# Expert output tiles: scaled on ScalarE and summed in DRAM by accumulating transfers, instead of summed in SBUF on VectorE

## The chip, the core and the metric

The kernel runs on one core of a Trainium2 chip. The core has a matrix engine (TensorE, PE in the profile), a vector engine (VectorE, DVE), an activation engine (ScalarE, ACT), a general-purpose engine (GpSimd, POOL) and a queue engine (SyncE, SP). Each executes its own instruction list in order, and waits on semaphores for the others. Sixteen DMA engines move data between DRAM and the on-chip memory (SBUF). The metric is device time in microseconds (us) for one execution.

## The reference, cut to what matters

```python
attn_out = attention(q, k, v, p)              # two small softmax attentions, 4 x 8 heads
x = attn_out as a 2304 x 512 matrix           # tokens x model width
h = x @ w_in;  g = h * cos(h);  x = g @ w_out # first feed-forward layer, 2048 wide
P = exp(logits - max), 8 rounds of row and column scaling   # 2304 x 8 gate, logits = x @ w_gate
out = zeros(2304, 512)
for e in range(8):                            # eight experts, 1024 wide, all of them for every token
    h = maximum(x @ w1[e], 0)
    ye = h @ w2[e]
    out += P[:, e:e+1] * ye
```

The change is about the last line: how the eight experts' results are scaled by the gate column and added up.

## The kernel before

Everything is float32 split into a high and a low part, so that each product is three matmuls (high x high, high x low, low x high). The first part of the program (attention and the first layer) has its last matmul (L562) at 403.9 us. The rest is the expert part, and the change lies in it alone.

**Units.** An expert's 1024 hidden columns are done in two halves, so there are 16 units (`u` from `U1` to `NU - 1`; `e, half = divmod(u - U1, 2)`). A unit goes over five token blocks `j`: four blocks of 512 tokens (`j` = 0 to 3) and a rest of 256 tokens (`j == NJ`). In a block, `g1_steps` makes the hidden activations in seven steps `n` = 0 to 6, each a call of `g1_mult` (12 matmuls, L726) followed by small VectorE and ScalarE work (L734, L735, L750, L755); the rest block uses `g1_rest` (L795) in two steps. The second matmul of an expert is done by `out_tile`: 12 matmuls of 512 columns (L830 to L832) make one output tile of 128 tokens x 512. A unit has 18 tiles: four for each of four blocks, two for the rest. The tiles of a block are made one block later: those of block `j` stand between the steps of block `j + 1` (after steps 1, 3, 4 and 5), and the two tiles of the rest block stand in block 0 of the next unit, after steps 1 and 3.

**Where output is summed.** `acc` (two SBUF tiles, `acc0` and `acc1`) holds the sum of all experts. Expert 0 writes it (ScalarE copy L836 in the first half, a VectorE add L838 in the second). Each later unit adds onto it with one VectorE instruction per tile, `scalar_tensor_tensor` on L842: `acc = psum * prob[:, t, e] + acc`. At the first half of expert 1 a `tensor_scalar` (L841) scales what expert 0 left. The last unit also writes each tile to the output in DRAM from SP's queue: one transfer for a tile of a block (L848), four transfers of 32 rows for a rest tile (L851), since its rows lie in four places; the very last tile is done in two parts of 256 columns.

**What sets the order.** The order is written by hand (`tc.manual_schedule()`); every engine gets its instructions in the order in which the program's lines are executed. Output tiles rotate over three PSUM banks. SP's queue carries the loads: `x_load` (L660) brings the two parts of one operand of `g1_mult` from DRAM (2 x 256 KB); it is issued after each `g1_mult`, into one of four slots, for the fourth `g1_mult` after it. The weights of the next unit are loaded at block 1 (L675, 4 x 256 KB; L212, 2 x 512 KB).

**What GpSimd does.** In the expert part it makes the low parts of the weights: `put` (L683) and `comb` (L686) for the first weights, and `w2_split` (L221) for the second ones, each of whose high parts ScalarE writes first (L682, L220). In the loop below, the splits of weight rows 2 and 3 of a unit stand in block 0 after the tiles of step 3 and in step 5 (`n in (3, 5)`); they are first read by the first tile of block 0, in block 1 after step 1. GpSimd issues no transfers before.

Of the kernel before, what the change touches and what calls it, by code (L numbers as in the profile page):

```python
# [13 lines left out]
AF = mybir.ActivationFunctionType  # L14
ALU = mybir.AluOpType
# [11 lines left out]
NU = U1 + U2  # L27
# [4 lines left out]
NJ = 4  # L32
# [71 lines left out]
def tile_kernel(ctx: ExitStack, tc: tile.TileContext, qT, kT, v, pT, w_in, w_out, w_gate, w1, w2, out):  # L104
    nc = tc.nc
# [17 lines left out]
    prob = const.tile([P, NT // P, E], F32, name="prob")  # L123
# [350 lines left out]
    def acc_cols(o, n):  # L474
        i, o = divmod(o, NT * KD // 2)
        return acc[i][:, o:o + n]
# [325 lines left out]
    def out_g2(u, j, i):  # L802
        parts = 2 if u == NU - 1 and j == NJ and i == 1 else 1
        for part in range(parts):
            out_tile(u, j, i, part, DM // parts)

    def out_rows(j, i):
        if j < NJ:
            r = HC * (2 * j + i // 2) + P * (i % 2)
            return out[r:r + P]  # L810
        return out.rearrange("(c r) d -> c r d", r=HC)[4 * i:4 * i + 4, HT:HC]

    def out_tile(u, j, i, part, width):
        t = 4 * j + i
        e, half = divmod(u - U1, 2)
        o = part * width
        ps = bank[:, 4 + counts["bank"] % 3, 0:width]
        counts["bank"] += 1
        for f in range(4):
            wh, wl = w_sb[u, 2, f]  # L820
            p, q = divmod(f, 2)
            if j < NJ:
                hi, lo = h_sb[u, j][q, i // 2]
                c = HT * p + P * (i % 2)
            else:
                hi, lo = h_sb[u, j][None, p]
                c = HT * q + P * i
            a, bq = hi[:, c:c + P], lo[:, c:c + P]
            wh, wl = wh[:, o:o + width], wl[:, o:o + width]
            nc.tensor.matmul(ps, lhsT=a, rhs=wh, start=(f == 0), stop=False)  # L830
            nc.tensor.matmul(ps, lhsT=a, rhs=wl, start=False, stop=False)  # L831
            nc.tensor.matmul(ps, lhsT=bq, rhs=wh, start=False, stop=(f == 3))  # L832
        dst = acc_cols(DM * t + o, width)
        if e == 0:
            if half == 0:
                nc.scalar.copy(dst, ps)  # L836
            else:
                nc.vector.tensor_tensor(out=dst, in0=ps, in1=dst, op=ALU.add)  # L838
            return
        if e == 1 and half == 0:  # L840
            nc.vector.tensor_scalar(dst, dst, prob[:, t, 0:1], None, ALU.mult)  # L841
        nc.vector.scalar_tensor_tensor(  # L842
            out=dst, in0=ps, scalar=prob[:, t, e:e + 1], in1=dst, op0=ALU.mult, op1=ALU.add
        )
        if u == NU - 1:
            rows = out_rows(j, i)
            if j < NJ:
                nc.sync.dma_start(out=rows[:, o:o + width], in_=dst)  # L848
            else:
                for c in range(4):  # L850
                    nc.sync.dma_start(  # L851
                        out=rows[c, :, o:o + width], in_=dst[32 * c:32 * c + 32, :]
                    )

# [76 lines left out]
    with tc.manual_schedule():  # L933
# [181 lines left out]
        for u in range(U1, NU):  # L1115
            for j in range(NJ + 1):
# [16 lines left out]
                i = 0  # L1133
# [76 lines left out]
```

## Time and profile before

| | |
|---|---|
| median of three runs | 1965.75 us (1965.14 to 1967.0) |
| the profiled execution: its own time | 1966.81 us |
| the profiled execution: span of the trace | 1965.0 us |
| TensorE (PE) busy | 1929.4 us, 98% of the span |
| VectorE / ScalarE / GpSimd busy | 49% / 32% / 26% of the span |
| granted TensorE clock, mean | 0.995 of full speed |
| DMA traffic | 319.08 MB, 162 GB/s on average |

The span is what the hardware profiler recorded between the first and the last instruction; the execution's own time lies 1.81 us above it. A busy share over the whole span mixes the parts of the program. What the change is worth is read from the expert part, from 634.9 us (the first L842, first tile of expert 1) to the end.

### The profile page before, as it was taken

The page shows a single profiled execution, that of the slowest core. Times are in us where ns is not written, and L with a number is a line of the kernel's source. Part 1 is how long each engine was busy: PE and PEld are TensorE (multiplying, and loading weights), DVE is VectorE, ACT ScalarE, POOL GpSimd, SP SyncE. Part 2 cuts the span into 40 slices and gives each one's busy share as a digit, 9 for nine tenths or more (in the row PEclk, how much of TensorE's full clock was granted, in tenths as well). Part 3 has the DMA queues.
Part 4 walks back from the last instruction along what each step waited for, and adds up shares of the span by engine and source line. Part 5 has one row for each costly group of instructions (what it writes and reads, how often), then busy time and mean ns, then how long its engine had stood idle before and what let it go on. Part 6 is the DMA issues. An engine that isn't in the chain of part 4 may idle for free.

```text
span 1965.0 us, 32232 instructions
## 1 busy us (share of the span) xinstructions
PE 1929.4 (98%) x13241; PEld 1739.3 (89%) x13241; DVE 964.8 (49%) x1439; ACT 621.7 (32%) x1062; POOL 516.4 (26%) x414
## 2 busy tenths in 40 slices
PE   7999999988999999999999999999999999999998
PEld 4799999977899898999989989898989898889897
DVE  6867776655544544343434444444434443434343
ACT  5877776633222212121212122222222121212110
POOL 3445554611221212121212131212122221212100
PEclk9999999999999999999999999999999999999999
DMA  8411111288464646455555556464647373736373
GB/s 296 151 46 53 55 54 34 81 262 260 138 214 148 207 153 194 161 190 166 188 179 165 182 161 197 147 213 130 219 125 234 109 237 118 236 117 231 117 228 102
DMA packets 287891, 319.08 MB, mean 162 GB/s; under 512 B 18432, under 2 KB 265088, under 8 KB 287744
## 3 DMA queue, kind: packets, MB, share of 16 engines
q1 hardware_dynamic: 287744, 317.02, 50.1%
q8 instruction: 104, 1.70, 0.4%
q14 instruction: 43, 0.35, 0.1%
HBM read 297.55 MB, written 19.40 MB: 161 GB/s over the span
## 4 chain that ended last, share of the span: by engine, by line
PE 93%; DVE 2%; ACT 2%; DMA 1%; issue 1%; POOL 1%; SPq 0%; ACTq 0%; DVEq 0%; POOLq 0%
PE bank L726 32%; PE bank L830 13%; PE bank L831 13%; PE bank L832 13%; PE bank L562 9%; PE bank L795 5%; PE bank L503 1%; PE bank L505 1%; PE bank L504 1%; PE bank L440 1%; DMA xl<-xd 1%; DMA k<-kT 1%; PE bank L866 0%; DVE xl L618 0%; DMA xd<-xl 0%
## 5 line engine op out<-in xcount | busy, mean ns | idle before, releaser
L726 PE MATMUL bank<-xh 128*128 128x256 f32 x1792 | 508.5, 284 | 2.8 <-DMA xh<-xd 2.6
L726 PE MATMUL bank<-xl,xh 128*128 128x256 f32 x1792 | 507.0, 283 | 1.6 <-DMA xl<-xd 1.6
L726 PE MATMUL bank<-xh,xl 128*128 128x256 f32 x1792 | 506.9, 283 | 0.0
L842 DVE SCALAR_TENSOR_TENSOR acc<-bank,prob,acc 128x512 f32<-128x512 f32 (+1 forms) x253 | 189.4, 749 | 364.4 <-PE bank L832 364.1
L726 PEld LDWEIGHTS bank<-xh 128*128 128x128 f32 x1792 | 340.9, 190 | 17.9 <-issue 4.7
L726 PEld LDWEIGHTS bank<-xl,xh 128*128 128x128 f32 x1792 | 341.1, 190 | 11.7 <-DMA xl<-xd 2.2
L726 PEld LDWEIGHTS bank<-xh,xl 128*128 128x128 f32 x1792 | 341.7, 191 | 0.0
L683 POOL TENSOR_TENSOR xl<-wraw,xh 128x512 fp32r<-128x512 f32 x128 | 167.2, 1321 | 649.0 <-ACT xh L682 469.2
L830 PE MATMUL bank<-whi,hreg 128*128 128x512 f32 (+1 forms) x822 | 324.0, 394 | 0.0
L831 PE MATMUL bank<-wlo,hreg 128*128 128x512 f32 (+1 forms) x822 | 323.6, 394 | 0.0
L832 PE MATMUL bank<-whi,hreg 128*128 128x512 f32 (+1 forms) x822 | 322.8, 393 | 0.0
L734 ACT ACTIVATE hreg<-c 128x512 fp32r<-128x512 f32 x137 | 86.6, 632 | 448.5 <-DVE c L750 448.5
L221 POOL TENSOR_TENSOR wlo<-raw,whi 128x512 fp32r<-128x512 f32 x64 | 82.8, 1294 | 510.7 <-ACT whi L220 510.7
L562 PE MATMUL bank<-hreg,whi 128*128 128x288 f32 x1024 | 187.1, 294 | 0.6 <-DVE acc L573 0.4
L832 PEld LDWEIGHTS bank<-whi,hreg 128*128 128x128 f32 x822 | 154.8, 188 | 35.6
L830 PEld LDWEIGHTS bank<-whi,hreg 128*128 128x128 f32 x822 | 155.0, 189 | 28.0
L831 PEld LDWEIGHTS bank<-wlo,hreg 128*128 128x128 f32 x822 | 155.0, 189 | 27.1
L562 PEld LDWEIGHTS bank<-hreg,whi 128*128 128x128 f32 x1024 | 152.8, 188 | 2.6 <-DVE rbuf L543 1.2
L735 DVE SCALAR_TENSOR_TENSOR hreg<-c,hreg 128x512 fp32r<-128x512 f32 x137 | 97.6, 712 | 99.5 <-ACT hreg L734 99.5
L831 PE MATMUL bank<-wlo,slot 128*128 128x512 f32 (+1 forms) x334 | 131.0, 392 | 0.0
L830 PE MATMUL bank<-whi,slot 128*128 128x512 f32 (+1 forms) x334 | 131.0, 392 | 0.0
L832 PE MATMUL bank<-whi,slot 128*128 128x512 f32 (+1 forms) x334 | 130.4, 391 | 0.0
(152 smaller groups left out, 2812.4 us busy)
## 6 DMA issues: line engine op xcount, KB each, us to landing
xh<-xd SPq DMA_DIRECT2D x444, 256.0 KB, 3.4
xl<-xd SPq DMA_DIRECT2D x444, 256.0 KB, 3.9
raw<-w SPq DMA_DIRECT2D x32, 512.0 KB, 5.7
wraw<-w SPq DMA_DIRECT2D x64, 256.0 KB, 5.5
raw<-w_in SPq DMA_DIRECT2D x16, 512.0 KB, 3.9
raw<-w_out SPq DMA_DIRECT2D x16, 512.0 KB, 3.5
xd<-xh SPq DMA_DIRECT2D x28, 256.0 KB, 3.9
xd<-xl SPq DMA_DIRECT2D x28, 256.0 KB, 3.9
```

Source lines behind the costliest of these rows:

```text
L221: nc.gpsimd.tensor_tensor(out=lo, in0=raw, in1=hi.bitcast(F32), op=ALU.subtract)
L440: nc.tensor.matmul(ps[64 * h:64 * h + 64, :], lhsT=pp_slot(j, b), rhs=w_sb[u, 1, j], start=True, stop=True,)
L562: nc.tensor.matmul(ps[:, di, 0:HC], lhsT=lhsT, rhs=rhs, start=(n in (0, 6)), stop=(n in (17, 23)),)
L683: nc.gpsimd.tensor_tensor(out=lo, in0=src, in1=hi.bitcast(F32), op=ALU.subtract)
L726: nc.tensor.matmul(dst, lhsT=w, rhs=t[:, k, :], start=start and p + k == 0 and w is a and t is th, stop=p + k == 2 and w is bq, skip_group ...
L734: nc.scalar.activation(hi, src, AF.Relu)
L735: nc.vector.scalar_tensor_tensor(out=lo, in0=src, scalar=0.0, in1=hi.bitcast(F32), op0=ALU.max, op1=ALU.subtract)
L795: nc.tensor.matmul(dst, lhsT=w, rhs=t, start=q + k == 0 and w is a and t is th, stop=q == 1 and k == KD - 1 and w is bq, skip_group_check= ...
L830: nc.tensor.matmul(ps, lhsT=a, rhs=wh, start=(f == 0), stop=False)
L831: nc.tensor.matmul(ps, lhsT=a, rhs=wl, start=False, stop=False)
L832: nc.tensor.matmul(ps, lhsT=bq, rhs=wh, start=False, stop=(f == 3))
L842: nc.vector.scalar_tensor_tensor(out=dst, in0=ps, scalar=prob[:, t, e:e + 1], in1=dst, op0=ALU.mult, op1=ALU.add)
```

## The change

From the second half of expert 1 on, a tile is no longer added onto `acc` by VectorE. ScalarE scales the PSUM tile by the gate column and writes it to the tile's place in `acc` (which is now only a staging place), and GpSimd issues a transfer with `accum_op=ALU.add` that adds it onto the rows of the output in DRAM. The first half of expert 1 still ends with `scalar_tensor_tensor`, and its tiles, which hold expert 0 and half of expert 1, are written to the output by plain transfers from SP's queue. The last unit has no transfers of its own on SP any more.

```diff
--- before.py
+++ after.py
@@ -837,20 +837,21 @@
             else:
                 nc.vector.tensor_tensor(out=dst, in0=ps, in1=dst, op=ALU.add)
             return
+        rows = out_rows(j, i)
+        parts = [(rows, dst)]
+        if j == NJ:
+            parts = [(rows[c], dst[32 * c:32 * c + 32, :]) for c in range(4)]
         if e == 1 and half == 0:
             nc.vector.tensor_scalar(dst, dst, prob[:, t, 0:1], None, ALU.mult)
-        nc.vector.scalar_tensor_tensor(
-            out=dst, in0=ps, scalar=prob[:, t, e:e + 1], in1=dst, op0=ALU.mult, op1=ALU.add
-        )
-        if u == NU - 1:
-            rows = out_rows(j, i)
-            if j < NJ:
-                nc.sync.dma_start(out=rows[:, o:o + width], in_=dst)
-            else:
-                for c in range(4):
-                    nc.sync.dma_start(
-                        out=rows[c, :, o:o + width], in_=dst[32 * c:32 * c + 32, :]
-                    )
+            nc.vector.scalar_tensor_tensor(
+                out=dst, in0=ps, scalar=prob[:, t, e:e + 1], in1=dst, op0=ALU.mult, op1=ALU.add
+            )
+            for rows, src in parts:
+                nc.sync.dma_start(out=rows[:, o:o + width], in_=src)
+            return
+        nc.scalar.activation(dst, ps, AF.Copy, bias=0.0, scale=prob[:, t, e:e + 1])
+        for rows, src in parts:
+            nc.gpsimd.dma_start(out=rows[:, o:o + width], in_=src, accum_op=ALU.add)
 
 
 
```

On GpSimd's list, the accumulating transfers stand between the weight splits. These are the rows of GpSimd before, around the start of the last unit (`xl` is the low part of a first-layer weight, `wlo` that of a second-layer weight; the last row is the split of rows 2 and 3 in block 0):

```order
L686 TENSOR_TENSOR wraw<-wraw 128x512
L683 TENSOR_TENSOR xl<-wraw,xh 128x2x256
L686 TENSOR_TENSOR wraw<-wraw 128x512
L221 TENSOR_TENSOR wlo<-raw_16407,whi 128x512 x2
L683 TENSOR_TENSOR xl<-wraw,xh 128x2x256 x4
L221 TENSOR_TENSOR wlo<-raw_16409,whi 128x512 x2
```

And these are the rows of GpSimd now, at the same place (`out<-acc` is an accumulating transfer; `acc_96` is `acc0`, `acc_1623` is `acc1`):

```order
L686 TENSOR_TENSOR wraw<-wraw 128x512
L854 DMA out<-acc_96 128x512
L221 TENSOR_TENSOR wlo<-raw_16698,whi 128x512
L854 DMA out<-acc_96 128x512
L221 TENSOR_TENSOR wlo<-raw_16698,whi 128x512
L854 DMA out<-acc_1623 128x512 x5
L683 TENSOR_TENSOR xl<-wraw,xh 128x2x256 x2
L854 DMA out<-acc_1623 128x512 x2
L683 TENSOR_TENSOR xl<-wraw,xh 128x2x256 x2
L854 DMA out<-acc_1623 32x512 x8
L221 TENSOR_TENSOR wlo<-raw_16700,whi 128x512 x2
```

The last two rows say that the eight 32-row transfers of the rest tiles now stand ahead of the splits of weight rows 2 and 3, which stood right behind the four `xl` rows before. Every transfer waits for ScalarE's scaling of its tile, and so for TensorE.

At the end of the program the transfers move from SP to GpSimd. SP's last rows before:

```order
L660 DMA xl<-xd 128x2x256
L848 DMA out<-acc_96 128x512
L660 DMA xh<-xd 128x2x256
L660 DMA xl<-xd 128x2x256
L848 DMA out<-acc_1623 128x512 x7
L851 DMA out<-acc_1623 32x512 x4
L851 DMA out<-acc_1623 32x256 x8
```

GpSimd's last rows now:

```order
L221 TENSOR_TENSOR wlo<-raw_16700,whi 128x512 x2
L854 DMA out<-acc_96 128x512 x9
L854 DMA out<-acc_1623 128x512 x7
L854 DMA out<-acc_1623 32x512 x4
L854 DMA out<-acc_1623 32x256 x8
```

The same 28 transfers close the program, twelve of them for the two rest tiles, but they are issued by another engine and add instead of overwrite.

## Rows read from the trace of the kernel before

**Rows 1.** Stretches: length, busy PE, PEld, DVE, ACT, POOL; granted clock, DMA share, GB/s.

```profile
634.00:1957.00 1323.00, 1322.56 (x8279) 1192.68 (x8278) 558.99 (x790) 267.07 (x458) 266.95 (x208) 1.00 0.55 176
1753.70:1849.40 95.70, 95.70 (x603) 86.38 (x602) 39.68 (x56) 19.78 (x34) 20.50 (x16) 1.00 0.54 176
```

**Rows 2.** What TensorE waited for, 634 to 1957 us: total, times, longest.

```profile
PE bank L726 <- DMA xl<-xd: 0.4, 1, 0.4
```

**Rows 3.** Groups by line in that unit, VectorE and GpSimd: busy, mean ns.

```profile
L842 DVE SCALAR_TENSOR_TENSOR acc<-bank,prob,acc 128x512 f32<-128x512 f32 x18 | 13.5, 751 | 26.8 <-PE bank L832 26.8
L221 POOL TENSOR_TENSOR wlo<-raw,whi 128x512 fp32r<-128x512 f32 x4 | 5.2, 1296 | 30.8 <-ACT whi L220 30.8
```

**Rows 4.** ScalarE groups that read a 128x512 PSUM tile, whole program.

```profile
L734 ACT ACTIVATE hreg<-bank 128x512 fp32r<-128x512 f32 x68 | 40.6, 597 | 233.4 <-PE bank L726 146.7 <-PE bank L795 86.6
L836 ACT COPY acc<-bank 128x512 f32<-128x512 f32 x18 | 10.5, 586 | 43.0 <-PE bank L832 43.0
```

**Rows 5.** SP's output transfers by line: issue ns, then landing times.

```profile
L851 SPq DMA_DIRECT2D out<-acc x12: 315/416/507, 1957.3 to 1962.6; - x12
DMA to landing us min/median/max: 1.5/1.6/2.0
...
L848 SPq DMA_DIRECT2D out<-acc x16: 332/350/351, 1880.0 to 1954.5; - x16
DMA to landing us min/median/max: 2.0/2.1/3.7
```

**Rows 6.** End of the program in time order, SP then VectorE.

```profile
1957.26 5.78 SPq L851 DMA_DIRECT2D out<-acc  x12
...
1956.48 0.75 DVE L842 SCALAR_TENSOR_TENSOR acc<-bank,prob,acc 128x512 f32<-128x512 f32 x1 [2.03 <-PE bank L832]
...
1959.28 0.48 DVE L842 SCALAR_TENSOR_TENSOR acc<-bank,prob,acc 128x256 f32<-128x256 f32 x1 [0.91 <-PE bank L832]
```

**Rows 7.** A unit's start in time order: rest tiles on VectorE, splits on GpSimd.

```profile
1768.02 0.75 DVE L842 SCALAR_TENSOR_TENSOR acc<-bank,prob,acc 128x512 f32<-128x512 f32 x1 [2.04 <-PE bank L832]
1773.64 0.75 DVE L842 SCALAR_TENSOR_TENSOR acc<-bank,prob,acc 128x512 f32<-128x512 f32 x1 [2.07 <-PE bank L832]
...
1772.27 1.29 POOL L221 TENSOR_TENSOR wlo<-raw,whi 128x512 fp32r<-128x512 f32 x1 [11.64 <-ACT whi L220]
1779.11 1.30 POOL L221 TENSOR_TENSOR wlo<-raw,whi 128x512 fp32r<-128x512 f32 x1 [5.55 <-ACT whi L220]
```

**Rows 8.** TensorE's first reads of those two splits, same unit.

```profile
1782.16 0.39 PE L831 MATMUL bank<-wlo,slot 128*128 128x512 f32 x1
...
1782.84 0.39 PE L831 MATMUL bank<-wlo,hreg 128*128 128x512 f32 x1
```

**Rows 9.** Chain of waits: start us, length us; three steps of 12 matmuls.

```profile
1797.52 4.27 PE bank L726 x36
```

**Rows 10.** DMA of that unit, SP's queue: packets, MB, share of 16 engines.

```profile
q1 hardware_dynamic: 16096, 16.78, 53.7%
```

**Rows 11.** One `x_load`: its issue, its landing, the matmul that needs it.

```profile
1799.38 0.47 SPq L660 DMA_DIRECT2D xl<-xd  x1
...
DMA to landing us min/median/max: 4.1/4.2/4.3
...
1805.93 0.28 PE L726 MATMUL bank<-xl,xh 128*128 128x256 f32 x1
...
1797.56 0.75 DVE L842 SCALAR_TENSOR_TENSOR acc<-bank,prob,acc 128x512 f32<-128x512 f32 x1 [0.71 <-PE bank L832]
```

**Rows 12.** ScalarE's waits on GpSimd (whole program), and one in block 2.

```profile
ACT xh L682 <- POOL wraw L686: 106.0, 32, 4.2
...
1805.59 0.62 ACT L682 CAST xh<-wraw 128x512 fp32r<-128x512 f32 x1 [4.03 <-POOL wraw L686]
1806.12 0.59 ACT L734 ACTIVATE slot<-bank 128x512 fp32r<-128x512 f32 x1
...
1821.57 0.59 ACT L755 COPY ta<-bank 128x512 f32<-128x512 f32 x1
```

## The prediction

> **What bounds the kernel now.** I read the stretches by engine first, to see which engine has no room. From 634 to 1957 us TensorE is busy 1322.56 of 1323.00 us, at a granted clock of 1.00, and one unit of 95.7 us shows no gap at all, while VectorE works 39.7 us of it, ScalarE 19.8 and GpSimd 20.5 [rows 1]. The list of TensorE's waits in that stretch has one line, 0.4 us for a load, and none for VectorE [rows 2]. So in the part that the change touches TensorE is the bound, and what is taken from VectorE is taken from an engine that nobody waits for. The change can gain nothing between 634 and 1957 us; it can only make something late, or move the end of the program. Three places matter: the end, the start of each unit, where GpSimd's splits have a due time, and the DMA engines.
>
> **VectorE and ScalarE.** Of the 253 executions of L842 the 18 of the first half of expert 1 stay, and 235 go: in a unit 18 x 751 ns = 13.5 us [rows 3]. ScalarE gets 235 scalings of a 128x512 PSUM tile. It has no such operation before; its copies and activations out of PSUM of that size take 586 and 597 ns [rows 4], so I take 0.6 us, 18 x 0.6 = 10.8 us a unit, ScalarE then at 30.6 of 95.7 us. PSUM banks come free 0.15 us earlier. Both go beside TensorE: term 0. What could be late is ScalarE's other work, because ScalarE waits for GpSimd's L686 in 32 places (106.0 us) and GpSimd would now stand in a transfer's issue before that L686. In block 2 the L682 at 1805.59 waits so, with an L734 right behind it that empties a PSUM bank at 1806.12. With a scaling done at about 1805.1, an issue of 1 us and an L686 of 1.3 us, that L734 comes at about 1808. The bank is written again in step 0 of the next block, whose copy L755 starts at 1821.57 after 1.4 us of matmuls [rows 9, 12], so 12 us of cover remain. Term 0; the cover is gone only if an issue took over 10 us.
>
> **The 24 plain writes of expert 1's first half** go out on SP, between loads. VectorE's instruction starts when the tile is done and takes 0.75 us [rows 3], SP's issue 0.35 [rows 5]: 1.1 us in all, under the 1.4 us of the next step's matmuls (4.27 / 3) [rows 9], behind which the next load is issued. A rest tile has four (0.35 + 3 x 0.48 more), up to 1.1 us late, against the 2.2 us of slack worked out below. Term 0.
>
> **The accumulating transfers on GpSimd.** 13 units have 24 each (16 of a whole tile, 8 of 32 rows), and the last tile adds 4: 316. Two prices are not in the trace: how long GpSimd stands in one issue (d), and how long the DMA engines work at one. For d the nearest rows are SP's issue, 0.35 us for a tile and 12 in 5.78 us (0.48 each) for the small ones [rows 5, 6], and GpSimd's own operation over 128 partitions, 1.3 us [rows 3]. I take d = 1.0 us, nearer to the latter, since GpSimd is the engine that does it: bounds 0.48 and 1.3. A unit then costs GpSimd 24 us on top of 20.5, 44.5 of 95.7: no bound by its sum.
>
> **The start of a unit** has the tightest due time. The rest tiles end at about 1768.0 and 1773.6 (where VectorE's L842 starts) [rows 7]; ScalarE needs 0.6 us each. Eight issues follow, four from 1768.6 on and four from 1774.2 on, and only then the two L221, 1.3 us each, that end at 1773.6 and 1780.4 now [rows 7]. TensorE reads the first at 1782.16 and the second at 1782.84 [rows 8]. With d = 1.0 the issues end at 1778.2; the second L221 cannot start before its high part (about 1779.1 as now), so both are ready by 1780.8, 2.0 us early. The point where it turns is 1768.6 + 8d + 2.6 = 1782.84, d = 1.45 us, just over my upper bound. Term 0.
>
> **The DMA engines.** In the unit the queue moves 16.78 MB in 53.7% of 95.7 us, which is 3.06 us a MB [rows 10]. The tiles are 18 x 0.262 = 4.72 MB, so 14.4 us more if a transfer that adds costs as much as a plain one: share 69%. If it costs twice that, 84%; three times, 99%. The Trainium skill speaks against the low price: "Collectives: The Full Stack", section on the bandwidth ceiling and the fold count, says that a reducing transfer reads two sources for one write and measures it at about half the rate of a copying one. By the page the share would be 84%, by the plain row 69%; no trace here has an adding transfer. The sum of shares is not all, since loads have due times too. The tightest repeating one is the load issued after step 6: issued at 1799.38, landed at most 4.3 us later, at 1803.7, needed by the matmul at 1805.93, a slack of 2.2 us [rows 11]. Beside it now runs the adding transfer of the tile that ended at 1797.56: scaled by 1798.2, issued by 1799.2, 0.8 us of all engines at the plain price and 1.6 at twice, which is the most that it can delay the load. Both are under 2.2; at about 2.75 times the plain price TensorE begins to wait. An adding transfer has two tiles to read where a plain one has one, so I take between one and two: term 0, upper bound worked out as a rival.
>
> **The end.** Before, SP starts the first of the last twelve transfers at 1957.26 and needs 5.78 us, to 1963.04, though VectorE is done at 1959.76 [rows 6]: the last landing is 1.6 us after the last issue began, at 1962.6 [rows 5]. After, the first tile ends at 1956.48 [rows 6], its scaling at 1957.1, and GpSimd issues twelve in a row: 12.0 us at d = 1.0, to 1969.1. That is 6.1 us later than 1963.04; for reading the old value back I add 0.5 us (bounds 0 and one more landing, 1.6). Term +6.6 us. At d = 0.48 and nothing for the reading back it is -0.2, at 1.3 and 1.6 it is +11.3.
>
> **Sum.** Against the profiled execution (span 1965.0, own time 1966.81) +6.6 is the only term. That execution is 1.06 us above the median, 1965.75, and I put the term on the median: 1972.4 us. A difference under 0.2% (3.9 us) cannot be told from none in this kernel.
>
> **Rivals.**
> *No slower (0.23).* GpSimd's issue is as cheap as SP's. The place is the end, the price 12 x (d - 0.48) plus the reading back, and it decides below d of about 0.75: then 12 x 0.27 + 0.5 = 3.7 us or less, time 1965.6 to 1969.7. For it: the shares leave GpSimd alone otherwise. Against: GpSimd is slow at all else in the rows (1.3 us where ScalarE has 0.6). The Trainium skill leans to this rival: "DMA: Bandwidth & Descriptors", section on the anatomy of a GpSimd transfer, puts most of its fixed 2 us into the landing's receipt and little into the issue. Faster by more than 3.9 us it could not be: with free issues the last tile, done at 1959.76, would still need a landing of about 2 us and end 2.4 us earlier than now. I give that 0.03.
> *GpSimd late at each unit's start (0.13).* d over 1.45 us, at 12 unit starts, each 8d + 2.6 - 14.2 us late. At d = 2.0 that is 4.4 us x 12 = 53, and the end adds 12 x 1.52 + 0.5 = 18.7: about 2037 us. At d = 1.6 it is 1.2 x 12 = 14 plus 13.9: 1994. For it: four small transfers in a row are just what an engine with a high fixed cost does badly. Against: needs a price above any row of GpSimd.
> *The DMA engines full (0.15).* An adding transfer at four times the plain price makes 51.4 + 57.8 = 109.2 us of DMA work in a unit of 95.7: 13.5 us x 13 = 175, time near 2147. At three times the sum just fits (94.7 us) and only the tight loads are late, 4 in a unit by some 0.2 us: 10 us more, 1983. For it: the reading back and the adding are priced nowhere here. Against: shares have room up to three times.
>
> **Chances and range.** The forecast, slower by 4 to 11 us with the units unchanged, has 0.46. Together with the two dearer rivals slower has 0.74, no difference 0.23, faster 0.03. If the units stay as they are the time is in 1965.5 to 1977.5. To hold 8 in 10 the range reaches over the milder part of both dearer rivals: 1965.5 to 2030.
>
> **What would show it.** Right: TensorE still without waits inside the units, VectorE about 176 us less busy (235 x 751 ns), ScalarE about 141 us more; on GpSimd's list twelve issues back to back from about 1957 on, 1 us apart, and a span that ends about 1.5 to 2 us after the last. Wrong: waits of TensorE for GpSimd's L221 at each unit's start (d over 1.45), or for the loads of L660, with landing times well above 4 to 5 us (transfers that add cost over 2.75 plain ones); or a last issue before 1966 us (d under 0.75).

## The result, and the profile after

| | before | changed |
|---|---|---|
| median | 1965.58 us (4 runs) | 1981.03 us (4 runs, 1976.06 to 1982.65) |
| profiled execution: own time / span | 1966.81 / 1965.0 us | 1982.65 / 1980.9 us |
| TensorE's last matmul ends | 1959.2 us | 1970.3 us |
| from there to the end of the span | 5.8 us | 10.6 us |

The ratio is 1.0073, with a 95% interval of 1.0054 to 1.0092: slower, by 15.5 us between the medians. The spans differ by 15.9 us, and the last two rows of the table split that: 11.1 us are lost before TensorE's last matmul, 4.8 us after it. The forecast was +6.6 us, all of it after the last matmul.

The page of the changed kernel, busy times and share of the span (part 1), the two DMA queues (packets, MB, share of 16 engines), and the two new groups of instructions:

```profile
PE 1933.1 (98%) x13241; PEld 1741.3 (88%) x13241; DVE 812.7 (41%) x1204; ACT 777.0 (39%) x1297; POOL 794.0 (40%) x730
...
q1 hardware_dynamic: 287552, 317.02, 49.5%
q0 software_dynamic: 35136, 61.36, 19.8%
HBM read 297.55 MB, written 80.74 MB: 191 GB/s over the span
...
L854 POOL DMA_DIRECT2D out<-acc x316 | 269.3, 1045 | 641.7 <-ACT acc L852 637.3
...
L852 ACT ACTIVATE acc<-bank,prob 128x512 f32<-128x512 f32 x235 | 161.0, 685 | 498.1 <-PE bank L832 498.1
```

ScalarE gained 155 us of work and GpSimd 278, as the change says. VectorE lost 152, less than the 176 of the 235 executions of L842 that went, because another line of it grew: L735 with both inputs in SBUF went from 712 to 845 ns (137 times) and from 726 to 878 ns (55 times), 27 us in all, while with one input in PSUM it stayed at 691. One such L735, at 1786.19 us beside GpSimd's issues and splits, took 1.96 us. TensorE waited for none of them.

The 61.36 MB of adding transfers took 19.8% of the 16 engines' span, 392 us, which is 6.39 us a MB; SP's queue took 49.5% for 317.02 MB, 3.09 us a MB. So a megabyte of adding transfers costs the engines 2.07 times as much as one on SP's queue.

The same stretch as in [rows 1], and TensorE's waits and those of its weight loads (PEld) in the units that follow adding transfers, 800 to 1975 us, where [rows 2] had 0.4 us once:

```profile
634.00:1957.00 1323.00, 1316.27 (x8218) 1185.16 (x8217) 407.35 (x556) 419.50 (x687) 532.28 (x509) 1.00 0.84 221
...
PE bank L726 <- DMA xl<-xd: 4.7, 9, 0.9
...
PEld bank L726 <- DMA xl<-xd: 7.7, 13, 1.1
```

The DMA share went from 0.55 to 0.84, and TensorE now waits for loads (`xl<-xd`, L660), about once a unit, never for GpSimd's splits. The chain of waits says where (start us, length us; three of the twelve such places from 723 us on). First the kernel before:

```profile
1679.15 4.35 DMA xl<-xd
```

That is the only such place in its chain after 500 us. The changed kernel:

```profile
1688.44 4.74 DMA xl<-xd
1693.23 1.56 PE bank L726 x11
...
1785.14 4.65 DMA xl<-xd
1789.83 1.58 PE bank L726 x11
...
1881.79 4.06 DMA xl<-xd
1885.90 1.57 PE bank L726 x11
```

Each piece is one load: the one that SP issues after step 4 of block 0. Between it and the step that reads it (step 1 of block 1) stand steps 5, 6 and 0 and no tile, because the previous unit has only two tiles for this block and both come after steps 1 and 3. Its margin before and after, in the unit of [rows 7]; first the kernel before, its landing times counted from the issue (at 1775.05 us for the high and 1775.45 for the low part, which is the one that took 3.1), the last matmul of the second rest tile, and the first matmul that needs the low part:

```profile
DMA to landing us min/median/max: 2.6/2.8/3.1
...
1773.21 0.39 PE L832 MATMUL bank<-whi,hreg 128*128 128x512 f32 x1
...
1779.23 0.28 PE L726 MATMUL bank<-xl,xh 128*128 128x256 f32 x1
```

Step 4 starts at 1773.44, when the tile is done. Four steps of 1.42 us follow (4, 5, 6 and 0), so step 1 starts at 1779.12, and its second matmul, at 1779.23, is the first to read the low part. That is 3.78 us after the issue. The low part landed at 1775.45 + 3.1 = 1778.55, 0.68 us in time. Now the same load in the changed kernel, with GpSimd's rows beside it (start, length):

```profile
1785.14 0.48 SPq L660 DMA_DIRECT2D xl<-xd  x1
...
DMA to landing us min/median/max: 3.5/4.1/4.6
...
1789.83 0.39 PE L726 MATMUL bank<-xl,xh 128*128 128x256 f32 x1 [0.75 <-DMA xl<-xd]
...
1778.75 3.21 POOL L854 DMA_DIRECT2D out<-acc  x4 [2.19 <-ACT acc L852]
1784.30 3.18 POOL L854 DMA_DIRECT2D out<-acc  x4 [2.34 <-ACT acc L852]
1786.32 2.96 POOL L221 TENSOR_TENSOR wlo<-raw,whi 128x512 fp32r<-128x512 f32 x1
1790.07 1.30 POOL L221 TENSOR_TENSOR wlo<-raw,whi 128x512 fp32r<-128x512 f32 x1 [0.79 <-ACT whi L220]
```

GpSimd starts the four adding transfers of the second rest tile 0.84 us before SP issues the low part. That lands at 1789.7, 1.5 us later than before relative to its issue, and TensorE waits 0.75 us. The other units agree. At the eleven unit starts from 818 to 1776 us the kernel before had the low part 2.9 to 3.2 us after its issue (once 4.3, its only wait); at the same starts in the changed kernel it takes 3.9 to 4.9 us, against the 3.78 that are there. From the second rest step of one unit to that of the next the kernel before takes 95.7 us and the changed one 96.4 (799.73 to 1860.23 us in eleven units); 0.69 x 11 = 7.6 us.

One unit start lost more: 99.3 us instead of 95.7, at the end of expert 1's first half, whose tiles are written by plain transfers on SP's queue. SP's rows, TensorE's, and the stretches behind the wait (columns as in [rows 1]):

```profile
721.02 1.75 SPq L850 DMA_DIRECT2D out<-acc  x4
722.88 0.38 SPq L660 DMA_DIRECT2D xh<-xd  x1
723.30 0.48 SPq L660 DMA_DIRECT2D xl<-xd  x1
...
727.83 0.38 PE L726 MATMUL bank<-xl,xh 128*128 128x256 f32 x1 [1.72 <-DMA xl<-xd]
...
728.00:730.00 2.00, 2.00 (x12) 2.00 (x12) 0.00 (x0) 0.00 (x0) 0.00 (x0) 0.57 0.92 288
730.00:732.00 2.00, 2.00 (x7) 1.57 (x7) 0.69 (x1) 0.00 (x0) 0.00 (x0) 0.58 1.04 363
```

The four writes of the rest tile stand in SP's list ahead of the same tight load. It leaves about 1.2 us late, and it lands 4.5 us after its issue instead of the 3.0 of the same place before: 2.7 us later in all, against about 0.7 of margin. Which of the transfers around it makes it land later no run separates. TensorE waits 1.7 us, and the granted clock then is 0.57 and 0.58 for 4 us (the level of 1.2 GHz for most of it), which adds about as much again. So the 11.1 us are 3.6 here and 7.6 in the eleven units, less 0.1 in the rest of the program.

The end, to be set beside [rows 6]: GpSimd's last row, and the landing of the last eight transfers (median, us).

```profile
1968.58 9.63 POOL L854 DMA_DIRECT2D out<-acc  x12 [1.86 <-ACT acc L852]
...
out<-acc POOLq DMA_DIRECT2D x8, 32.0 KB, 4.5
```

Twelve issues take 9.63 us where SP needed 5.78, 0.80 us each. The 4.5 us are counted from the start of an issue that itself stands behind the others: the longest L854 lasts 4.13 us.

### The profile page after: what moved, and what is told of

Its sections match the earlier page's. It is cut to its first block, busy times and chain, and to the rows that moved or that the text cites. A ratio compares the mean times of both kernels' runs of the same rounds, so it can differ in the third digit from the quotient of the medians.

```text
span 1980.9 us, 33055 instructions
## 1 busy us (share of the span) xinstructions
PE 1933.1 (98%) x13241; PEld 1741.3 (88%) x13241; DVE 812.7 (41%) x1204; ACT 777.0 (39%) x1297; POOL 794.0 (40%) x730
## 3 DMA queue, kind: packets, MB, share of 16 engines
q1 hardware_dynamic: 287552, 317.02, 49.5%
q0 software_dynamic: 35136, 61.36, 19.8%
HBM read 297.55 MB, written 80.74 MB: 191 GB/s over the span
## 4 chain that ended last, share of the span: by engine, by line
PE 75%; DMA 3%; DVE 1%; POOL 1%; ACT 1%; issue 0%; SPq 0%; POOLq 0%; DVEq 0%; ACTq 0%
PE bank L726 29%; PE bank L830 13%; PE bank L831 13%; PE bank L832 13%; PE bank L795 5%; DMA xl<-xd 3%; PE bank L562 1%; POOL out L854 0%; DVE xl L618 0%; PE bank L867 0%; SPq L660 0%; DMA xd<-xl 0%; DVE hreg L735 0%; DVE tx L611 0%; ACT hreg L734 0%
## 5 line engine op out<-in xcount | busy, mean ns | idle before, releaser
L854 POOL DMA_DIRECT2D out<-acc x316 | 269.3, 1045 | 641.7 <-ACT acc L852 637.3
L852 ACT ACTIVATE acc<-bank,prob 128x512 f32<-128x512 f32 x235 | 161.0, 685 | 498.1 <-PE bank L832 498.1
L683 POOL TENSOR_TENSOR xl<-wraw,xh 128x512 fp32r<-128x512 f32 x128 | 174.7, 1440 | 158.5 <-ACT xh L682 136.5
L750 DVE TENSOR_TENSOR c<-bank,tc 128x512 f32<-128x512 f32 x128 | 88.1, 688 | 226.0 <-PE bank L726 226.0
L221 POOL TENSOR_TENSOR wlo<-raw,whi 128x512 fp32r<-128x512 f32 x64 | 102.6, 1603 | 182.7 <-ACT whi L220 175.0
L735 DVE SCALAR_TENSOR_TENSOR hreg<-c,hreg 128x512 fp32r<-128x512 f32 x137 | 115.8, 845 | 112.9 <-ACT hreg L734 112.9
L735 DVE SCALAR_TENSOR_TENSOR hreg<-bank,hreg 128x512 fp32r<-128x512 f32 x68 | 47.0, 691 | 263.1 <-ACT hreg L734 263.1
```

The costliest lines, as they stand in the source:

```text
L221: nc.gpsimd.tensor_tensor(out=lo, in0=raw, in1=hi.bitcast(F32), op=ALU.subtract)
L683: nc.gpsimd.tensor_tensor(out=lo, in0=src, in1=hi.bitcast(F32), op=ALU.subtract)
L735: nc.vector.scalar_tensor_tensor(out=lo, in0=src, scalar=0.0, in1=hi.bitcast(F32), op0=ALU.max, op1=ALU.subtract)
L750: nc.vector.tensor_tensor(out=out, in0=ps, in1=other, op=ALU.add)
L852: nc.scalar.activation(dst, ps, AF.Copy, bias=0.0, scale=prob[:, t, e:e + 1])
L854: nc.gpsimd.dma_start(out=rows[:, o:o + width], in_=src, accum_op=ALU.add)
```

## Experiments

Theory A: the load after step 4 of block 0 lands late because the rest tiles' adding transfers run beside it, at twice the price of plain ones; the rest of the loss is GpSimd's issues at the end. (The expectations of e3 and e6 were worked out with a margin of 0.3 us for this load; the rows above give 0.68.) Each rival is named in the expectation of the run that tests it. The kernel before was run beside each group: 1966.27 us (18 runs) beside the first four, 1966.72 (33 runs) beside the last four.

**e1: the rest tiles' adding transfers held back to the end of block 3.** The list `held` and the function that issues what it holds are left out here.

```diff
+            if j == NJ and u < NU - 1:
+                held.append((rows[:, o:o + width], src))
+            else:
                 nc.gpsimd.dma_start(out=rows[:, o:o + width], in_=src, accum_op=ALU.add)
...
+                    if j == 3 and n == 6:
+                        release_held()
```

> The eight adding transfers of the rest tiles are held back from block 0 of the next unit to the end of block 3, the rest is as in the changed kernel. Theory A (the load issued after step 4 of block 0, which has no tile between it and its matmul, lands late because the rest tiles' adding transfers run beside it): the about 0.9 us wait at each unit start goes, TensorE's last matmul comes 9 to 11 us earlier, time about 1971. Rival B (the DMA engines are simply fuller, whatever stands beside that load): the waits stay, 1979 to 1983. Rival C (GpSimd's splits L221 come late behind the eight issues): the same gain as A, but then the waits of the changed kernel would name L221.

Measured 1974.16 us (6 runs), ratio 1.0039 (1.0026 to 1.0053). TensorE's waits from 700 to 1955 us, of which the stretch of the changed kernel had 6.4 us:

```profile
PE bank L726 <- DMA xl<-xd: 1.1, 2, 1.0
...
700.00:1955.00 1255.00, 1253.78 (x7851) 1130.41 (x7850) 357.25 (x506) 407.56 (x666) 514.10 (x499) 1.00 0.85 221
```

The DMA share is as high as in the changed kernel (0.85), the bytes and prices are the same, and of the waits at the unit starts behind adding transfers one of 0.2 us is left; the low part of the tight load lands at most 3.0 us after its issue in seven of twelve units again, and within 4.0 in the others. Rival B falls, and C with it, since no wait names L221 in either kernel. The median came down 7 us, not 9 to 11: the unit behind the plain writes keeps part of its loss (97.3 us), which this edit does not touch; the wait of 1.0 us above is there.

**e2: a tile between the load and its matmul.** The second rest tile is made after step 4 instead of 3, and the splits stand in steps 4 and 5.

```diff
-                places = (1, 3, 5) if prev is None else (1, 3, 4, 5) if j < NJ else (0, 0, 1, 1)
+                places = (1, 3, 5) if prev is None else (1, 4) if j == 0 else (1, 3, 4, 5) if j < NJ else (0, 0, 1, 1)
...
-                    if j == 0 and n in (3, 5):
+                    if j == 0 and n in ((3, 5) if prev is None else (4, 5)):
```

> The second rest tile is made after step 4 of block 0 instead of after step 3 (and the split behind it one step later), so that a tile of 2.8 us stands between that load and its matmul; all transfers stay. Theory A and rival B both say that the load now has 3 us of slack and the waits go: about 1970.5, the end alone left (+5). Rival C (late splits) says that it gets no better or worse, since the splits are due at the same time and begin 1.4 us later: 1981 or more.

Measured 1972.46 us (7 runs), ratio 1.0033 (1.0021 to 1.0044). TensorE's waits from 700 to 1955 us:

```profile
PE bank L726 <- DMA xl<-xd: 0.9, 1, 0.9
PE bank L832 <- DVE slot L735: 0.5, 1, 0.5
```

The second rest tile's adding transfers move with the tile: they start 3.4 us after the issue of the tight load instead of 0.84 us before it. But the loads land as late as before the edit (median 5.0 us from 800 to 1900 us, as in the changed kernel), the tight one even later, 4.9 to 6.0 us after its issue, and its waits in these units are gone, because it has 2.8 us more. The 0.9 us are the unit behind the plain writes. The other wait is new: one of the longer L735 of VectorE, 0.5 us. The last matmul ends at 1960.5 us and the span at 1971.1: 10.6 us, the changed kernel's end.

**e3: plain transfers from GpSimd.** Without `accum_op` the output holds only the last unit's part.

```diff
-            nc.gpsimd.dma_start(out=rows[:, o:o + width], in_=src, accum_op=ALU.add)
+            nc.gpsimd.dma_start(out=rows[:, o:o + width], in_=src)
```

> The same 316 transfers from GpSimd, written over the output instead of added (so the output holds only the last unit's part). Theory A with the doubled cost of adding as its reason: the load is late by half as much, with 0.3 us of slack to cover, so the waits fall to 3 to 5 us in all; the end gets 1 to 2 us shorter; about 1973. Rival D (it is the second queue, or GpSimd's issues, whatever the transfers do): waits and end stay, 1979 to 1983. The DMA share of GpSimd's queue falls from 19.8% to about 10% under A.

Measured 1969.35 us (10 runs), ratio 1.0017 (1.0007 to 1.0027). GpSimd's queue, the issue times of L854 (min, median, max in ns), the landing of those transfers, and GpSimd's last row:

```profile
q0 software_dynamic: 20096, 61.36, 10.3%
...
L854 POOL DMA_DIRECT2D out<-acc x316: 498/542/745, 732.6 to 1964.7; - x158
...
DMA to landing us min/median/max: 1.7/2.8/6.5
...
1959.24 5.98 POOL L854 DMA_DIRECT2D out<-acc  x12 [2.23 <-ACT acc L852]
```

The same bytes cost 202.7 us of the engines, 3.30 us a MB: adding costs 1.93 times as much on the same queue. The tight load lands within 3.3 to 4.2 us, the eleven units take 95.8 us each, and twelve issues take 5.98 us, nearly SP's 5.78. TensorE's waits from 700 to 1955 us are 1.5 us, 1.2 of them behind the plain writes; 3 to 5 were expected, with too small a margin. So the higher price is in three places, all of them the adding: the engines' time, GpSimd's issue (542 ns against 881 in the changed kernel) and the landing (2.8 us against 5.0). Rival D falls.

**e4: VectorE scales.**

```diff
-        nc.scalar.activation(dst, ps, AF.Copy, bias=0.0, scale=prob[:, t, e:e + 1])
+        nc.vector.tensor_scalar(dst, ps, prob[:, t, e:e + 1], None, ALU.mult)
```

> VectorE scales the tile into its staging place instead of ScalarE, the transfers stay as in the changed kernel. Theory A: which engine scales is of no weight, 1977 to 1983. Rival E (ScalarE's 235 added instructions delay its other work and TensorE with it): most of the 15 us goes, about 1970.

Measured 1977.0 us (4 runs, 1976.19 to 1978.79), ratio 1.0058 (1.004 to 1.0075), whose interval overlaps that of the changed kernel. Most of the loss stays (10.7 of 15.5 us), so rival E does not explain it. In its trace TensorE's waits for the tight load are fewer, though (from 700 us on 3.1 us in 4 places against 6.4 in 10), and a unit takes 96.1 us. GpSimd's second four transfers start only up to 0.1 us nearer to the load there, and the load lands in 3.3 to 3.8 us in seven of the eleven units from 819 to 1780 us. Why it lands earlier was not settled; with 3.78 us to land in, tenths decide.

**e5: e2, with the very last tile in one part**, so that 8 adding transfers close the program instead of 12.

```diff
-        parts = 2 if u == NU - 1 and j == NJ and i == 1 else 1
+        parts = 1
```

> The version with the tile between, and the very last tile done in one part of 512 columns, so that the program ends with 8 adding transfers instead of 12. If the rest of the loss is GpSimd's issue of adding transfers at the end (0.80 us each, back to back), four issues less take 3.2 us off, less about 0.3 us for the larger last scaling: 1969 to 1970 against 1972.5. If it is the landing of the last one alone, nothing is gained: 1972 to 1973.

Measured 1969.6 us (10 runs), ratio 1.0021 (1.001 to 1.0031). GpSimd's last row:

```profile
1960.32 6.42 POOL L854 DMA_DIRECT2D out<-acc  x8 [1.87 <-ACT acc L852]
```

Eight issues, 0.80 us each, and from the last matmul to the end 7.8 us instead of 10.6. What the end loses goes with GpSimd's issues, one after the other.

**e6: the kernel before with the tile between.** The edit is that of e2, made in the kernel before.

> A control: the kernel before, with the second rest tile made after step 4 of block 0. If the tight load costs the kernel before nothing (its slack is 0.3 us and it lands in time in all but one unit), the time is that of before within 0.1%. If the place of the tile is worth something by itself, then that is part of what the changed kernel with the tile between won, and this one is faster by up to 10 us.

Measured 1965.04 us (11 runs), ratio 0.9992 (0.9983 to 1.0001): no difference that can be told. TensorE is busy without a gap from 700 to 1955 us, but there was hardly one to close. So what e2 won, it won back from the adding transfers, not by the place of the tile alone.

**e7: the kernel before, its last twelve transfers from SP and ScalarE in turn.**

```diff
-                    nc.sync.dma_start(
+                    (nc.sync, nc.scalar)[c % 2].dma_start(
                         out=rows[c, :, o:o + width], in_=dst[32 * c:32 * c + 32, :]
                     )
```

> The kernel before, with its last twelve transfers issued from SP and ScalarE in turn. If SP's issues are what its end waits for (12 in 5.78 us, while VectorE is done 3.3 us before the last of them), the end comes about 2.3 us earlier, 0.1%: just what five rounds can tell. If the landing is what counts, no change.

Measured 1964.63 us (11 runs), ratio 0.9989 (0.998 to 0.9998). SP's last row; ScalarE's queue has its own six at the same time:

```profile
1956.56 3.31 SPq L851 DMA_DIRECT2D out<-acc  x6
```

From the last matmul to the end it takes 3.6 us instead of 5.8, so that end waited for the issues of one queue.

**e8: the kernel before with both, e6 and e7.**

> The kernel before with both: the tile between, and the last transfers from two queues. Expected is the sum of the two, 2 to 3 us faster than before; if the two stand in each other's way, less.

Measured 1962.95 us (11 runs), ratio 0.9976 (0.9967 to 0.9985). It is the fastest of all: 0.24% under the kernel before, and under every version with adding transfers. The 3.8 us between the medians are a little more than the 2 to 3 expected.

## Why the prediction was right or wrong

**The direction was right, for less than half of the reason.** The sum had one term of +6.6 us, and the runs show two: +4.8 at the end and +11.1 in the units. The favoured case, the units unchanged and 1965.5 to 1977.5 us, did not come. The time lies in the range only because that was stretched to 2030 us for two rivals, neither of which came as it was described; that it held is in part luck.

**No gain from VectorE: right.** TensorE waited for no VectorE instruction before, and e4 shows that the engine that scales is not where most of the loss lies. A scaling takes 685 ns, not 600. VectorE got 152 us less busy, not 176, since its L735 grew, at no cost here.

**GpSimd's issue: right in kind, a little too dear.** 0.80 us back to back, between the bounds 0.48 and 1.3. The splits at the unit's start were ready in time, as worked out: no wait of TensorE names them.

**The end: right place, mis-sized.** The issues cost 9.63 - 5.78 = 3.9 us more, not 6.1. The rest is 0.9 us instead of the 0.5 for the reading back: the first issue starts 0.3 us later against TensorE's last matmul, and from the end of the last issue to the end of the span 2.7 us pass instead of 2.0. In e3, which reads nothing back, these are still 2.4, so the reading back itself is about 0.2. Together 4.8 instead of 6.6. e3 and e5 show that the issues are the larger part.

**The DMA engines' price: right.** Between one and two times the plain price was taken; 2.07 was measured against SP's queue, 1.93 against the same queue (e3), and the share came out at 0.84. "Collectives: The Full Stack", in the section of the Trainium skill on the bandwidth ceiling and the fold count, states half the rate for a transfer with two sources, there the reducing step of a ring of cores; e3 agrees, 6.39 us a MB against 3.30.

**The failed step: "The tightest repeating one is the load issued after step 6".** It isn't. The load issued after step 4 of block 0 has only steps 5, 6 and 0 before its own, three steps without a tile, and it landed 0.68 us in time, not 2.2. The 1.6 us worked out as the most that an adding transfer can delay a load were near the mark: 1.5 in the unit shown, 0.7 to 1.9 in ten of the eleven, so as a bound they were a little low. But they were set against the wrong slack. 1.5 us against 0.68 leaves a wait, and 0.8 us, the plain price, about fits (e3: 95.8 us a unit, against 95.7). e1 takes the collision away and e2 the tightness, and in both the waits in these units all but go; this is shown.

**The same slack failed a second time, in the plain writes.** "Up to 1.1 us late, against the 2.2 us of slack" had the lateness of the issue about right (1.2 us), and the slack wrong. It also took the landing as unchanged, and that was 1.5 us longer; the 2.7 us of both would have passed even the 2.2. The wait is 1.7 us, and with the lower clock behind it the unit loses 3.6 us. This is read from the trace; no run takes the plain writes away.

**The rivals.** *GpSimd late* did not happen, its point being 1.45 us of issue. *The DMA engines full* did not happen either (0.84), though its milder part, tight loads late, is what did, at 2.07 times the plain price where it wanted three. *No slower* falls, though narrowly, with the issue of 0.80 us against its 0.75; the section of "DMA: Bandwidth & Descriptors" (the Trainium skill) on the anatomy of a GpSimd transfer, which leaned to it, holds better for the plain transfers of e3 (0.54 us of issue) than for adding ones (0.88).

## What to carry to other kernels

When a change adds DMA traffic beside a saturated engine, the average share says little: here it was 0.84, and loads still came late. List every load with its issue and its first reader, take the one with the least margin at the boundaries of the loops, where the usual filler work is missing, and set the new transfer against that one. By these runs an adding transfer counts as two plain ones for the engines, and as one and a half to two of the same queue in issue and landing. Where a program ends with many small transfers, count the issues on one queue: they can set the end, as e5 and e7 show.

## What the runs showed of the hardware

The counter of HBM reads did not move (297.55 MB before and after), though 61.36 MB of old values had to be read back; the doubling shows only in the queue's share and in its packets, 35136 against 20096 in e3. A single wait of 1.72 us on TensorE was followed by 4 us at a granted clock of 0.57 to 0.58, while the wait of 0.75 us at 1789 us left it at 1.00 (both for 1788 to 1792 and for 1792 to 1796 us).
